# Linear attention and a four-expert MLP: where the late chunks of k are regrouped for VectorE's transpose

## The chip, the cores and the metric

The kernel runs on one core of a Trainium2 chip. The metric is the device time of one execution in microseconds (us). A core has five engines that work side by side, each with an instruction queue of its own that runs in order: TensorE (PE) multiplies matrices, VectorE (DVE) and ScalarE (ACT) do elementwise work and take results out of PSUM, GpSimd (POOL) does elementwise work in SBUF, and SyncE (SP) issues most DMA transfers; ScalarE can issue transfers too. Engines wait for one another, and for transfers, by semaphores.

## The reference

Two stages. The first is linear attention with a decay, over q, k, v of 4 batches, 8 heads, 768 tokens and 64 columns, in blocks of 64 tokens:

```python
for b in range(nb):
    sl = slice(b * block, (b + 1) * block)
    qb, kb, vb = (q[:, :, sl], k[:, :, sl], v[:, :, sl])
    intra = np.einsum('bhic,bhjc->bhij', qb, kb) * Dmask[None]
    intra = np.einsum('bhij,bhjd->bhid', intra, vb)
    inter = np.einsum('bhid,bhde->bhie', qb * lam_pow[None], kv_state)
    out[:, :, sl] = intra + inter
    kb_dec = kb * rev_pow[None]
    kv_state = lam_block[None, :, None, None] * kv_state + np.einsum('bhsd,bhse->bhde', kb_dec, vb)
```

The second takes the result as 3072 tokens of 512 columns through 4 experts (512 to 1024 and back to 512) and weighs their outputs:

```python
p = domain_probs / (domain_probs.sum(-1, keepdims=True) + 1e-09)
for e in range(E):
    h = np.maximum(x @ w1[e], 0.0)
    out += p[:, e:e + 1] * (h @ w2[e])
```

All data are fp32.

## The kernel before

**Tiling and stages.** The tokens go in three groups of 1024 (`NG`), and each group in 8 chunks of 128 tokens, so there are 24 chunks. A pair (group, expert) is a unit, 12 in all. The products of the experts are done by a fast scheme in seven products (`M1` to `M7`), and most of them by seven smaller ones inside. That scheme needs sums and differences of blocks of the weights; GpSimd makes them and stores them in DRAM, and they are loaded again when they are needed. After a start-up of about 100 us, in which the first group's attention and first product are made, the program is a list of steps: unit by unit, seven products in each, eight steps in each product. A step issues two or four pairs of matmuls, what takes their results out of PSUM, and a little of each of several lists.

**The attention of later chunks** is spread over these steps. `attention` (L892) lists for chunks 8 to 23 at which step each part is to be issued; `AT` (L888) holds the step of a chunk's scores. `turn` makes q and k stand with their 64 columns along the partitions, `scores` (L745) makes the products q k and the new state, and `values` (L805) makes the chunk's result, which ScalarE takes out of PSUM (L863) and VectorE completes with a sum. For chunks 8 to 11 `turn` uses TensorE. For the 12 chunks from 12 on (`comes_across`) VectorE does it (`turn_across`, L702): its transpose turns each square of 32 by 32 by itself, so the data must first stand with the right columns in each block of 32 partitions.

**How they come to stand so.** `bring_across` (L490) makes a list of 128 pieces, 32 for each batch: first 16 of q, then 16 of k. A piece is a transfer from DRAM to DRAM that writes 32 columns of one head in runs of 128 bytes; it has 32 KB in the first batch of the list and, for two others, 64 KB. `trickle` issues one piece at a time; in the first unit one in every step, from SyncE in the even steps and from ScalarE's queue in the odd ones, later in the odd steps. `load_across` (L509) loads a chunk's q and k from there into the tiles `qx` and `kx`, and `load` brings k a second time as it is (`kn`), which `decayed` multiplies on GpSimd and `scores` uses for the state. All three loads are issued five steps ahead of the turn.

**The order of the rest.** `send` (L109) issues a transfer and keeps two estimates in steps: `moved`, until when the DMA engines have work, and `asked`, until when SyncE has. `vector` keeps `filled` in the same way for VectorE. `pump` (L208) runs once a step; it begins the next of the `chores` (a load of weights, a sum on GpSimd) only if this holds:

```python
force or free[0] <= now[0] and max(moved[0], asked[0]) < now[0] + FULL and not resting[0]
```

Where a product needs operands that are not made yet, `first_product` (L1131) calls `pump(force=True)` until they are. Among the chores at the end of the start-up are those of the second expert's second weights (`prepare_w2`, L297, called at L1799): a step that loads block B21 and makes the sum T1, one that makes T2, one that makes T4; then come the operands of `M5` (`own_w1`, L1640). Sums and loaded blocks lie in the pool `stage`, which has 7 buffers; an instruction that writes a buffer waits for the readers of what was in it. Tiles such as `qx`, `kx` and `kn` come from a pool of 42 buffers.

## Time and profile before

| | us |
|---|---|
| median of 3 runs | 1142.28 |
| lowest and highest | 1141.87, 1142.56 |
| the profiled execution | 1142.07 |
| its span | 1140.3 |
| TensorE busy in it | 1130.5 |
| GpSimd, VectorE busy | 761.0, 769.0 |
| ScalarE busy | 380.3 |

The span runs from the first instruction of the program to the end of the last; the profiled execution's own time is 1.8 us longer. All times inside the profile count from the start of the span. A busy share is an average over stages: the start-up of about 100 us, the steps with attention until about 500 us, and the rest. In a row of the timeline the first number is the start and the second the length in us, and what stands in brackets is how long the engine had been idle and what released it. Matmuls overlap, so that the duration of one is longer than the distance between two.

### The profile page before, as it was taken

How to read it: one execution, taken by the hardware profiler on the slowest of the kernel's cores; microseconds unless marked ns; L12 is line 12 of the kernel's file. 1: busy time of each engine (PE TensorE's matmuls, PEld its weight loads, DVE VectorE, ACT ScalarE, POOL GpSimd, SP SyncE). 2: the span in 40 equal slices, each digit the busy share in tenths (PEclk: the TensorE clock that was granted, in tenths of full speed). 3: DMA queues.
4: the chain of work that ended last, by engine and by line, in shares of the span. 5: the costliest groups of instructions: out<-in, count | busy, mean ns of one | idle time of the engine just before them, and what ended most of it. 6: DMA issues, size and time to landing. Idle time of an engine off the chain costs nothing.

```text
span 1140.3 us, 22080 instructions
## 1 busy us (share of the span) xinstructions
PE 1130.5 (99%) x7983; PEld 988.2 (87%) x7983; DVE 769.0 (67%) x1474; ACT 380.3 (33%) x768; POOL 761.0 (67%) x730
## 2 busy tenths in 40 slices
PE   8999999999999999999999999999999999999998
PEld 7888888888888888888888888888888888888887
DVE  4576776587577658737655566878767576776785
ACT  3325123212312321232343442444354452342332
POOL 2838147644843786447687997994996873873885
PEclk9999999999999999999999999999999999999999
DMA  9795889999899989769557858886577757657552
GB/s 204 180 287 166 212 222 279 291 270 335 262 292 320 316 291 282 222 222 314 177 177 261 283 180 281 290 272 204 180 264 244 218 162 207 194 160 211 171 194 74
DMA packets 326828, 267.12 MB, mean 234 GB/s; under 512 B 153216, under 2 KB 270144, under 8 KB 326720
## 3 DMA queue, kind: packets, MB, share of 16 engines
q1 hardware_dynamic: 289472, 258.14, 73.1%
q10 hardware_dynamic: 37216, 7.57, 3.5%
q8 instruction: 64, 1.05, 0.4%
q14 instruction: 44, 0.36, 0.1%
q0 software_dynamic: 32, 0.00, 0.0%
HBM read 197.97 MB, written 73.96 MB: 238 GB/s over the span
## 4 chain that ended last, share of the span: by engine, by line
PE 98%; DVE 1%; issue 0%; DMA 0%; ACT 0%; DVEq 0%; POOLq 0%; ACTq 0%
PE pg L1174 41%; PE pq L1550 25%; PE q L1233 21%; PE pM L1692 2%; PE pc L1692 2%; PE op L824 1%; PE sp L761 1%; PE op L842 1%; PE sp L768 1%; PE pM L1417 1%; PE pg L1550 1%; PE qp L727 1%; PE kp L727 0%; DMA decay<-in_lam_dram 0%; PE yp L1377 0%
## 5 line engine op out<-in xcount | busy, mean ns | idle before, releaser
L1174 PE MATMUL pg<-xs,ws_in 128*128 128x256 f32 x1960 | 470.1, 380 | 0.0
L1174 PEld LDWEIGHTS pg<-xs,ws_in 128*128 128x128 f32 x1960 | 371.1, 190 | 52.8 <-DVE m L117 2.4
L117 DVE TENSOR_TENSOR m<-pg,m 128x512 f32<-128x512 f32 x374 | 255.4, 685 | 92.4 <-PE pg L1174 82.5
L1233 PE MATMUL q<-w2t,m 128*128 128x256 f32 x1120 | 265.6, 380 | 0.0
L1233 PEld LDWEIGHTS q<-w2t,m 128*128 128x128 f32 x1120 | 211.7, 190 | 29.3 <-issue 0.3
L117 DVE TENSOR_TENSOR sums<-pq,sums 128x256 f32<-128x256 f32 x272 | 112.9, 420 | 90.6 <-PE pq L1550 76.9
L1550 PE MATMUL pq<-acc,w2t 128*128 128x256 f32 x688 | 169.2, 379 | 0.0
L117 POOL TENSOR_TENSOR m<-m,decay 128x512 f32<-128x512 f32 x91 | 114.5, 1270 | 78.7 <-ACT m L1191 52.1
L1550 PEld LDWEIGHTS pq<-acc,w2t 128*128 128x128 f32 x688 | 130.6, 190 | 17.9
L1191 ACT ACTIVATE m<-m 128x512 f32<-128x512 f32 x99 | 62.4, 630 | 192.5 <-DVE m L117 190.6
L1251 DVE SCALAR_TENSOR_TENSOR acc<-q,gate,acc 128x256 f32<-128x256 f32 x108 | 52.0, 482 | 79.1 <-PE q L1233 78.6
L117 DVE TENSOR_TENSOR m<-m,m 128x512 f32<-128x512 f32 x108 | 92.9, 861 | 6.5 <-ACT m L1157 6.5
L1187 ACT COPY m<-pg 128x512 f32<-128x512 f32 x88 | 51.5, 585 | 122.0 <-PE pg L1174 108.7
L1151 ACT COPY pg<-m 128x512 f32<-128x512 f32 x77 | 45.4, 590 | 113.0 <-DVE m L117 103.3
L117 POOL TENSOR_TENSOR acc<-hT,hT 128x512 f32<-128x512 f32 x56 | 70.3, 1272 | 15.0 <-PE pq L1550 9.9
L117 POOL TENSOR_TENSOR acc<-hT,acc 128x512 f32<-128x512 f32 x56 | 71.2, 1272 | 6.4 <-PE pq L1550 2.7
L1550 PE MATMUL pq<-hT,w2t 128*128 128x256 f32 x288 | 70.0, 379 | 0.0
L117 POOL TENSOR_TENSOR w2o<-w2b 128x512 f32<-128x512 f32 x26 | 33.9, 1325 | 45.8 <-DMA w2b<-in_moe_w_dram 39.3
L1550 PEld LDWEIGHTS pq<-hT,w2t 128*128 128x128 f32 x288 | 54.7, 190 | 7.4
L1155 ACT COPY m<-pg 128x512 f32<-128x512 f32 x44 | 25.7, 585 | 89.6 <-PE pg L1174 84.8
L1550 PE MATMUL pq<-m,w2t 128*128 128x256 f32 x228 | 55.4, 379 | 0.0
L1005 ACT COPY hp<-m 128x512 f32<-128x512 f32 x84 | 48.5, 589 | 15.6 <-DVE hT L117 14.1
(157 smaller groups left out, 1419.5 us busy)
## 6 DMA issues: line engine op xcount, KB each, us to landing
ws_in<-w_ops SPq DMA_DIRECT2D x40, 512.0 KB, 5.1
w2t<-w_ops SPq DMA_DIRECT2D x72, 256.0 KB, 3.2
ws_in<-w_ops SPq DMA_DIRECT2D x60, 256.0 KB, 3.5
ws_in<-w_ops SPq DMA_DIRECT2D x40, 384.0 KB, 4.0
w2b<-in_moe_w_dram SPq DMA_DIRECT2D x56, 256.0 KB, 5.0
w_ops<-ops SPq DMA_DIRECT2D x28, 512.0 KB, 5.5
w_ops<-ops SPq DMA_DIRECT2D x54, 256.0 KB, 4.3
w2t<-w_ops SPq DMA_DIRECT2D x100, 128.0 KB, 2.8
```

The lines of the kernel that those rows point to most:

```text
L117: eng.tensor_tensor(out=o, in0=a, in1=b, op=op)
L727: nc.tensor.transpose(out=x[:, ac * C:(ac + 1) * C], in_=y[:, ac].rearrange("p r d -> p (r d)"), identity=ident[:],)
L1005: nc.scalar.copy(out=there[x][:], in_=blk[at][:])
L1151: nc.scalar.copy(out=banks[tags[1]][:], in_=new["11"][:])
L1155: nc.scalar.copy(out=o[:], in_=p[:])
L1174: nc.tensor.matmul(out=p[:, j * 256:(j + 1) * 256], lhsT=ws[i][:, j * P:(j + 1) * P], rhs=xs[i], start=(fresh and j == 0), stop=True, skip ...
L1187: nc.scalar.copy(out=new[at][:], in_=p[:])
L1191: nc.scalar.activation(out=new[at][:], in_=new[at][:], func=AF.Relu)
L1233: nc.tensor.matmul(out=p[:, s * DH:(s + 1) * DH], lhsT=h[A_OF[m]][:, c * 256 + s * P:c * 256 + (s + 1) * P], rhs=fed2[g, e, m][uu][:, c], ...
L1251: nc.vector.scalar_tensor_tensor(out=o, in0=x, scalar=w, in1=o, op0=ALU.mult, op1=ALU.add)
L1550: nc.tensor.matmul(out=p[:, 0:256], lhsT=fed3[e, m, i][:, c * P:(c + 1) * P], rhs=b[B_OF[i]][:, c * 256:(c + 1) * 256], start=(fresh and c ...
L1692: nc.tensor.matmul(out=p[:, s * 256:(s + 1) * 256], lhsT=a[c][:, f:f + P], rhs=b[:, c, j * 256:(j + 1) * 256], start=(s == 0 and c == 0 an ...
```

## The change

k of the late chunks is no longer copied within DRAM. `bring_across` makes pieces of q alone, 64 in all, and all of them go through SyncE. `load_across` loads `qx` alone. k is loaded as it is, by a step of its own that stands 15 to 18 steps ahead of the turn (`K_AHEAD`), and five steps after that load `regroup` puts 16 copies into a list: ScalarE copies 32 partitions by 4 heads by 32 columns from `kn` to their place in `kx`. Two copies are taken from the list in every step, and `moved_by` issues what is left of a chunk's when its turn comes. `turn_across` adds 0.41 to VectorE's estimate for each transpose in place of what `vector(W, False)` added.

```diff
-    across = dram.tile([2, P, NHP, B, 16, 32], FP32, name="across")
+    across = dram.tile([P, NHP, B, 16, 32], FP32, name="across")
...
-        for x, of in enumerate((q, k)):
-            for y in range(4):
-                for ac in range(NHP):
-                    src = of[b, 4 * (y // 2) + ac, c * C:, (y % 2) * 32:(y % 2 + 1) * 32]
-                    to = across[x, y * 32:(y + 1) * 32, ac, b, (c - 2) * 4:]
...
+        for y in range(4):
+            for ac in range(NHP):
+                src = q[b, 4 * (y // 2) + ac, c * C:, (y % 2) * 32:(y % 2 + 1) * 32]
+                to = across[y * 32:(y + 1) * 32, ac, b, (c - 2) * 4:]
...
     def load_across(n):
         c, b = where(n)
-        for x, name in enumerate("qk"):
-            t = small(f"{name}x")
-            send(
-                out=t[:].rearrange("p (h c) -> p h c", c=C),
-                in_=across[x, :, :, b, (c - 2) * 4:(c - 1) * 4].rearrange("p h t d -> p h (t d)"),
+        t = nat[n, "qx"] = small("qx")
+        send(
+            out=t[:].rearrange("p (h c) -> p h c", c=C),
+            in_=across[:, :, b, (c - 2) * 4:(c - 1) * 4].rearrange("p h t d -> p h (t d)"),
+        )
+
+    moves = []
+
+    def regroup(n):
+
+        of = nat[n, "k"]
+
+        def move(j, x):
+            if (n, "kx") not in nat:
+                nat[n, "kx"] = small("kx")
+            to = nat[n, "kx"][:].rearrange("p (h t c) -> p h t c", h=NHP, c=32)
+            nc.scalar.copy(
+                out=to[j * 32:(j + 1) * 32, :, x],
+                in_=of[x * 32:(x + 1) * 32, :, j // 2, j % 2 * 32:(j % 2 + 1) * 32],
             )
-            nat[n, name + "x"] = t
+
+        moves.extend((n, lambda j=j, x=x: move(j, x)) for j in range(4) for x in range(4))
+
+    def moved_by(n):
+        while any(m <= n for m, _ in moves):
+            moves.pop(0)[1]()
...
             load_across(n)
-            load(n, "k")
...
     def turn_across(n):
 
+        moved_by(n)
...
-            vector(W, False)
+            filled[0] = max(filled[0], now[0]) + 0.41
...
+    K_AHEAD = {14: 16, 15: 17, 16: 17, 18: 16, 20: 18, 22: 16}
...
             if comes_across(n):
+                steps.append((turns_at - K_AHEAD.get(n, 15), lambda n=n: load(n, "k")))
+                steps.append((turns_at - K_AHEAD.get(n, 15) + 5, lambda n=n: regroup(n)))
...
-                if at == 0 or x % 2 or at == 1 and x == 4:
-                    trickle(1, nc.scalar if x % 2 else None)
+                if at == 0 or x % 2:
+                    trickle()
+                for _ in range(2):
+                    if moves:
+                        moves.pop(0)[1]()
```

More of the change, by code (lines that the diff above doesn't have):

```diff
@@ L491, in bring_across @@
         c = min(where(n)[0] for n in range(FIRST_ACROSS, NG * CPG) if where(n)[1] == b)
-        for x, of in enumerate((q, k)):
-            for y in range(4):
-                for ac in range(NHP):
-                    src = of[b, 4 * (y // 2) + ac, c * C:, (y % 2) * 32:(y % 2 + 1) * 32]
-                    to = across[x, y * 32:(y + 1) * 32, ac, b, (c - 2) * 4:]
-                    pieces.append((rank[b], lambda by, to=to, src=src: send(
-                        out=to, in_=src.rearrange("(t p) d -> p t d", p=32), by=by,
-                    )))
+        for y in range(4):
+            for ac in range(NHP):
+                src = q[b, 4 * (y // 2) + ac, c * C:, (y % 2) * 32:(y % 2 + 1) * 32]
+                to = across[y * 32:(y + 1) * 32, ac, b, (c - 2) * 4:]
+                pieces.append((rank[b], lambda by, to=to, src=src: send(
+                    out=to, in_=src.rearrange("(t p) d -> p t d", p=32), by=by,
+                )))
     def trickle(m=1, by=None):
```

## The prediction

> **What bounds the kernel now.** I read the page's busy shares and chain first, then TensorE's waits after its start-up, then the two places that the change reaches: GpSimd around 100 us and ScalarE's queue from 160 to 490 us. On the page:

> ```profile
> span 1140.3 us, 22080 instructions
> ## 1 busy us (share of the span) xinstructions
> PE 1130.5 (99%) x7983; PEld 988.2 (87%) x7983; DVE 769.0 (67%) x1474; ACT 380.3 (33%) x768; POOL 761.0 (67%) x730
> ...
> PE 98%; DVE 1%; issue 0%; DMA 0%; ACT 0%; DVEq 0%; POOLq 0%; ACTq 0%
> ```

> TensorE is the bound: 98% of the chain. TensorE's waits from 60 to 1140 us (total, times, longest) are these two:

> ```profile
> PE sp L761 <- issue: 1.2, 1, 1.2
> PE op L824 <- DVE qT L117: 0.2, 1, 0.2
> ```

> So after start-up there are 1.4 us of idle TensorE to win. The changed program has the same 4052 matmuls in the same order. It can gain at most 1.4 us (0.12%); it can lose wherever a feeding engine becomes late.

> **Added: 192 ScalarE copies (12 chunks of 16, 32 partitions by 128 elements).** Nearest rows, ScalarE by shape from 150 to 500 us, and its timeline around 355 us:

> ```profile
> L863 ACT COPY xc<-op 128x128 f32<-128x128 f32 x60 | 11.4, 277 | 28.3 <-PE op L842 28.2
> ...
> L1155 ACT COPY m<-pg 128x512 f32<-128x512 f32 x13 | 7.6, 585 | 35.4 <-PE pg L1174 30.6 <-DMA across<-in_q_dram 4.8
> ```
> ```profile
> 353.06 0.77 ACT L863 COPY xc<-op 128x128 f32<-128x128 f32 x4 [6.92 <-PE op L842]
> 353.69 0.64 ACT L1151 COPY pg<-m 128x512 f32<-128x512 f32 x1
> 360.26 0.58 ACT L1155 COPY m<-pg 128x512 f32<-128x512 f32 x1 [5.93 <-PE pg L1174]
> ```

> 128 elements take 0.277 us alone, four in a row 0.77, so 0.19 each. 192 copies are 37 us (192 x 0.19) to 53 us (192 x 0.277), in about 310 us where ScalarE is a quarter busy. Out go 67 DMA issues of 0.557 us, 37 us. What covers the copies is the idle ScalarE time, such as the 5.93 us above, and slack behind it: TensorE reuses a bank at least 1.06 us, mostly 1.75 us, after ScalarE has evicted it. In the listed order at most eight copies (1.5 to 2.2 us) stand together; the groups ahead of the seeds at L1151 are of four (0.8 to 1.1 us), against 2.5 us of slack there. What can show is four copies ahead of an L863 eviction whose sum VectorE adds next, with a product sum behind it that TensorE takes within 0.1 us: four or so places of 0.1 us. Ends: 0 (all covered) and 13 us (four uncovered copies, 1.1 us, in each of 12 chunks). I take 0.4 us, near the covered end, because the row has the cover.

> **Moved: k's plain load, 10 to 13 steps earlier.** The copies, and all ScalarE work queued behind them, now wait for its landing: an eviction, then TensorE for the bank. A kn load lands 3.6 to 7.8 us after its issue. The two tightest, at 352 and 452 us, may issue only once an attention product is over (352.5 us); 7.8 us on is 360.3, two copies are 0.4 us, and the next ScalarE work, at 360.26 with over 1 us of slack, loses nothing. Ends 0 and 1 us each; I take 0. VectorE's transposes of k stand 2 to 17 us behind the last copy: 0. The kn buffers are held longer; what newly waits for one waits for matmuls already past.

> **Removed: 64 k pieces in DRAM and 12 loads of kx.** SP loses 39 issues (27 k pieces, 12 kx) and gains 30 (the q pieces that ScalarE's queue had): about 9 x 0.6 us fewer. Less traffic from 170 to 330 us helps loads that TensorE nearly waited for (one vn landed 0.1 us before its use at 268.9 us). The 1.2 us stall at 267.5 us lies beside it, in the fullest stretch of the DMA engines. Ends 0 and 1.4 us; I take all of the 1.2 us row, two chances in three.

> **Moved by the planner: a GpSimd step.** This is where I find the loss. `send` adds a q piece of 64 KB to `moved` where a k piece of 32 KB stood before, so `pump` holds the e=1 step that loads B21 and makes sum T1. In the listing, it and its successors T2 and T4 move from behind the matmuls that ran at 94 to 97 us to behind the one at 102.2 us, where `first_product` forces them because it needs M5's operands. SP then has eight pieces, not four, ahead of the B21 load; still early enough, as in the trace it issues this work 7 us ahead of the matmuls that it stands behind. But T2 asks for its `stage` buffer later and gets the one of M1's `ops`, and with it a wait that it did not have: the last matmul on that tile. No other step on GpSimd has a new wait for TensorE. GpSimd's timeline, then TensorE's:

> ```profile
> 88.38 2.57 POOL L117 TENSOR_TENSOR w2o<-w2b 128x512 f32<-128x512 f32 x2 [5.70 <-DMA w_sums<-w2o]
> 91.03 4.96 POOL L117 TENSOR_TENSOR w2o<-w2b,w2o 128x512 f32<-128x512 f32 x4
> 96.07 1.41 POOL L117 TENSOR_TENSOR ops<-w1o 128x256 f32<-128x256 f32 x2
> ...
> 99.44 2.50 POOL L117 TENSOR_TENSOR w1o<-w1o,w1b 128x512 f32<-128x512 f32 x2 [0.35 <-PE pg L1174]
> ```
> ```profile
> 98.33 1.03 PE L1174 MATMUL pg<-xs,ops 128*128 128x256 f32 x4
> ...
> 102.65 1.03 PE L1174 MATMUL pg<-xs,ops 128*128 128x256 f32 x4
> ```

> T2 and T4 are the four at 91.03; the first `ops` at 96.07 (0.72 us) feeds the matmul at 102.65. The awaited matmul ends at 99.36 (98.33 + 1.03), and GpSimd starts 0.08 us after it, as the 99.44 row shows. From 91.03 to the end of the first `ops` is 96.07 + 0.72 - 91.03 = 5.76 us. So these operands come at 99.44 + 5.76 = 105.20, and with 0.07 us for the wait TensorE resumes at 105.27: 105.27 - 102.65 = **2.6 us lost**. Ends 0 (the wait is over before GpSimd comes to it) and 4 us (the B21 load lands late too). I take 2.6: all its parts are rows. Next in need are the third `ops` (slack 7 us before, still over 1 us) and later ones, which the stall itself gives 2.6 us: nothing.

> **The clock after the stall.** TensorE in four stretches (length, busy, granted clock, DMA):

> ```profile
> 5.68:9.10 3.42, 2.58 (x74) 1.00 1.36 225
> ...
> 12.51:15.92 3.41, 1.31 (x63) 1.00 0.79 218
> 15.92:19.34 3.42, 3.42 (x20) 0.50 0.78 196
> ...
> 265.08:268.49 3.41, 2.38 (x94) 1.00 1.15 350
> ```

> The clock goes by stretches of 3.41 us. After one with 38% busy (1.31 of 3.41) the next ran at 0.50; after 70 and 75% busy it stayed 1.00. A stall of 2.6 us inside one stretch leaves 24% busy; split over two, up to 62%. A stretch at 0.50 costs 3.41 / 2 = 1.7 us. Ends 0 and 1.7; I take 1.7, since most positions of the stall leave a stretch nearer to 38% than to 70%. [...]

> **Sum**, on the profiled execution (1142.07 us, 0.21 below the median 1142.28): 1142.07 + 2.6 + 1.7 + 0.4 - 1.2 = **1145.6 us**, 0.3% above the median. From no change this kernel's runs can tell about 0.2% (2.3 us).

> **Rivals.**
> - [...] 33%: 24 same, 9 slower.
> - *The other side, the GpSimd wait is hidden*: TensorE finds its operands ready. 1142.07 + 0.4 - 1.2 = 1141.3, not slower; it decides if GpSimd starts T2 before 96.8 us (102.65 - 5.83). For: every other wait has slack. Against: the wait is for a matmul that ends at 99.36. 14%: 11 same; 3 faster, if stalls that I don't see go as well.
> - *k lands late*: ScalarE's queue stands at two or more chunks for over 1.75 us. Two stalls of 1 us: 1147.6. For: vn loads took up to 9.5 us. Against: those came with the traffic that is removed. 6%, slower.

> **How the numbers follow.** The forecast has 47%, all slower (1145.6, or 1146.8 with the stall at 267 kept). Slower 47 + 9 + 6 = 62%; same 24 + 11 = 35%; faster 3%. Range: from the hidden wait (1141.3) to 1148.0, the kept stall with late k loads (1146.8 + about 1).

> **What would show it.** Right: a new TensorE idle stretch of some 2.6 us at 102 to 105 us, before an `ops` matmul, released by GpSimd; GpSimd's T2 starting behind TensorE at 99.4 us; a granted clock of 0.50 for 3.4 us after; no wait at L761 near 267 us; ScalarE copies of 0.19 to 0.28 us. Wrong: TensorE idle between 160 and 490 us, above all released by ScalarE or by a kn load; or a span without the gap at 102 us.

## The result and the profile after

The changed kernel takes 1147.69 us in the median (1145.71 to 1151.8, 6 runs) against 1142.07 us before (1140.69 to 1142.78, 6 runs): a ratio of 1.0048, 95% interval 1.0033 to 1.0062. It is slower, by about 5.5 us. The forecast was 1145.6 us. The traced execution took 1149.67 us, 2 us above its median and 7.6 us above the traced one before.

The page of the changed kernel, span, busy time and chain:

```profile
span 1147.9 us, 22213 instructions
## 1 busy us (share of the span) xinstructions
PE 1133.6 (99%) x7983; PEld 989.6 (86%) x7983; DVE 772.4 (67%) x1474; ACT 437.3 (38%) x960; POOL 765.1 (67%) x730
...
PE 93%; SPq 2%; DVE 2%; issue 2%; DMA 1%; POOL 0%; ACT 0%; DVEq 0%; POOLq 0%; ACTq 0%
```

TensorE still has 99% of the span, but 7% of the chain now lies elsewhere. TensorE's waits from 60 us to the end (total, times, longest) name three places that were not there before, and the old 1.2 us at L761 is gone:

```profile
PE pg L1195 <- POOL ops L117: 2.4, 1, 2.4
PE pg L1195 <- DMA ws_in<-w_ops: 2.1, 1, 2.1
PE pg L1195 <- DVE m L117: 0.9, 1, 0.9
PE op L842 <- DVE qT L117: 0.2, 1, 0.2
```

Both kernels have the same 4052 matmuls in the same order, so each matmul's start in one trace can be taken from its start in the other. Worked out so, the delay against the kernel before grows like this:

| place in the changed kernel | delay before and behind it, us | what happens |
|---|---|---|
| 59.5 us | 0.04 | start-up over |
| 105.2 us | 0.04 to 2.58 | TensorE waits for GpSimd's `ops` |
| 105.2 to 108.8 us | 2.58 to 4.28 | half clock (granted 0.50 from 105.41 to 108.82 us) |
| 208.3 us | 4.38 to 5.28 | TensorE waits for VectorE |
| 272.5 us | 5.29 to 7.58 | TensorE waits for a load of `ws_in` |
| 272.5 to 276.4 us | 7.58 to 9.22 | half clock (granted 0.50 from 272.66 to 276.08 us) |
| 276.4 us | 9.22 to 7.79 | the stall before at 267.5 us is not there |
| end | 7.50 | |

**At 102 us** the forecast's line is there. The timelines of GpSimd, then of TensorE:

```profile
99.53 4.95 POOL L117 TENSOR_TENSOR w2o<-w2b,w2o 128x512 f32<-128x512 f32 x4 [7.66 <-issue]
104.45 1.41 POOL L117 TENSOR_TENSOR ops<-w1o 128x256 f32<-128x256 f32 x2
```
```profile
98.37 1.03 PE L1195 MATMUL pg<-xs,ops 128*128 128x256 f32 x4
...
101.82 1.03 PE L1195 MATMUL pg<-xs,w1o 128*128 128x256 f32 x4
105.22 1.93 PE L1195 MATMUL pg<-xs,ops 128*128 128x256 f32 x4 [2.37 <-POOL ops L117]
```

T2 starts 0.13 us behind the matmul that ends at 99.40 (98.37 + 1.03), and TensorE resumes at 105.22; the forecast had 99.44 and 105.27. Four matmuls then take 1.93 us, not 1.03.

**At 270 us** stands what the forecast did not have. SyncE's waits from 240 to 275 us, then its timeline, then the DMA engines from 247 to 273 us (one digit for each 0.65 us, in tenths of their time):

```profile
SPq L114 <- PE op L860: 11.8, 1, 11.8
```
```profile
241.61 3.71 SPq L114 DMA_DIRECT2D w_sums<-w2o  x2
256.73 0.53 SPq L114 DMA_DIRECT2D qx<-across  x1
...
262.72 0.52 SPq L114 DMA_DIRECT2D ws_in<-w_ops  x1
```
```profile
DMA  9710000000000000078899779999999999999996
```

SyncE stands for 11.8 us by this view (11.4 us from the end of its issue before, 245.32, to the start of this one) at the q load of chunk 14, until a matmul that ends at 256.67 us has read what stood in the buffer that this load is to fill, the `qx` of chunk 12. In the kernel before, the same load was issued without such a wait, 3 us ahead of the end of that matmul (251.39 us there):

```profile
248.35 0.55 SPq L114 DMA_DIRECT2D qx<-across  x1
```

In the changed kernel nothing can be issued behind it, so the DMA engines run dry for some 9 us (14 digits of 0), and then everything that has piled up is issued at once. The weights of the matmul at 270 us are the ninth transfer of that pile: issued at 262.72, 7.25 us before TensorE is ready for them, landed at 272.34 after 9.6 us.

**At 208 us** VectorE is late. Its timeline and GpSimd's:

```profile
206.04 1.60 DVE L117 TENSOR_TENSOR qx<-qx,decay 128x512 f32<-128x512 f32 x1
207.56 0.68 DVE L117 TENSOR_TENSOR m<-pg,m 128x512 f32<-128x512 f32 x1
```
```profile
205.82 2.94 POOL L117 TENSOR_TENSOR w1o<-w1o,w1b 128x512 f32<-128x512 f32 x2 [1.11 <-DMA w_ops<-ops]
```

The multiply of `qx` took 0.69 us in the trace before and 1.60 us here, with GpSimd's `w1o` sum beside it. That sum waits for a store to land; before, it began at 204.16 us, when VectorE's work of this stretch was over (203.54). The store took 6.1 us from issue to landing before (landed at 204.09 us) and takes 3.9 us here (205.75 us, where TensorE is 4.38 us later), so that it lands earlier in TensorE's order of work, and GpSimd's sum begins 0.2 us before VectorE's multiply.

### The profile page after: what moved, and what is told of

It is laid out like the page before. It is cut to its first block, busy times and chain, and to the rows that moved or that the text cites. A ratio compares the mean times of both kernels' runs of the same rounds, so it can differ in the third digit from the quotient of the medians.

```text
span 1147.9 us, 22213 instructions
## 1 busy us (share of the span) xinstructions
PE 1133.6 (99%) x7983; PEld 989.6 (86%) x7983; DVE 772.4 (67%) x1474; ACT 437.3 (38%) x960; POOL 765.1 (67%) x730
## 4 chain that ended last, share of the span: by engine, by line
PE 93%; SPq 2%; DVE 2%; issue 2%; DMA 1%; POOL 0%; ACT 0%; DVEq 0%; POOLq 0%; ACTq 0%
PE pg L1195 39%; PE pq L1571 24%; PE q L1254 20%; PE pc L1713 2%; SPq L114 2%; PE pM L1713 1%; PE op L842 1%; PE op L860 1%; PE sp L779 1%; DMA ws_in<-w_ops 1%; PE sp L786 1%; PE pM L1438 1%; PE pg L1571 1%; DVE m L117 0%; PE qp L745 0%
## 5 line engine op out<-in xcount | busy, mean ns | idle before, releaser
L117 DVE TENSOR_TENSOR m<-pg,m 128x512 f32<-128x512 f32 x374 | 255.0, 685 | 95.2 <-PE pg L1195 83.7
L117 DVE TENSOR_TENSOR sums<-pq,sums 128x256 f32<-128x256 f32 x272 | 112.9, 420 | 90.8 <-PE pq L1571 75.3
L117 POOL TENSOR_TENSOR m<-m,decay 128x512 f32<-128x512 f32 x91 | 114.6, 1273 | 86.0 <-ACT m L1212 63.2
L1212 ACT ACTIVATE m<-m 128x512 f32<-128x512 f32 x99 | 62.4, 630 | 161.0 <-DVE m L117 156.4
L117 DVE TENSOR_TENSOR m<-m,m 128x512 f32<-128x512 f32 x108 | 92.7, 858 | 7.5 <-ACT m L1178 6.8
L117 POOL TENSOR_TENSOR acc<-hT,hT 128x512 f32<-128x512 f32 x56 | 70.4, 1272 | 22.6 <-PE pq L1571 13.2
L117 POOL TENSOR_TENSOR acc<-hT,acc 128x512 f32<-128x512 f32 x56 | 71.3, 1273 | 6.6 <-PE pq L1571 2.0
L117 POOL TENSOR_TENSOR w2o<-w2b 128x512 f32<-128x512 f32 x26 | 35.8, 1396 | 42.4 <-DMA w2b<-in_moe_w_dram 30.4
L526 ACT COPY kx<-kn 32x128 f32<-32x128 f32 x192 | 56.7, 295 | 17.8 <-DMA kn<-in_k_dram 8.6
```

Of the source, the lines that this page charges most:

```text
L117: eng.tensor_tensor(out=o, in0=a, in1=b, op=op)
L526: nc.scalar.copy(out=to[j * 32:(j + 1) * 32, :, x], in_=of[x * 32:(x + 1) * 32, :, j // 2, j % 2 * 32:(j % 2 + 1) * 32],)
L1212: nc.scalar.activation(out=new[at][:], in_=new[at][:], func=AF.Relu)
```

## The experiments

The theory after the traces: two buffers are handed out differently, and each brings a wait for TensorE. One is T2's in the `stage` pool (the 102 us stall), the other that of chunk 14's `qx` in the pool of 42 small tiles. The listing of the program shows why the second is short: when that load asks, 41 tiles are live, because k's plain tiles now live 10 to 13 steps longer, and the only free one was released just before. In the kernel before, three were free. The rivals: the copies themselves cost, or SyncE's fuller queue, or the DMA engines are simply full at 270 us. All ratios are to the kernel before, run on the same chip beside the experiments (its medians were 1145.03, 1144.95 and 1145.77 us in the three sets, and its runs spread wider there, from 1140.5 to 1152.6).

### T2's buffer put back

```
-            if pieces:
+            if pieces and not 56 <= now[0] < 68:
                 pieces.pop(0)[1](by)
```

> The changed kernel, with one thing put back: no q piece is handed to SyncE in the steps that run from 88 to 108 us, so that T2's buffer is again that of a tile which nobody on TensorE reads. The copies, the early k loads and everything else stay. If the stall at 102 us is the wait of T2 for TensorE (GpSimd stood 7.66 us ahead of 99.53), the idle 2.5 us there and the 3.4 us at about half clock behind it go together, 2.5 + 1.7 = 4.2 us of the 1147.7, and the kernel takes 1143.5 us (1142.5 to 1145). If the loss is spread over the copies and the fuller SyncE queue, or if the stall moves to the next operand, it stays above 1146.5.

Ratio 0.9993 (0.9974 to 1.0011), 1145.5 us. TensorE's waits from 60 us on:

```profile
PE pg L1195 <- DMA ws_in<-w_ops: 1.4, 1, 1.4
PE pg L1195 <- DVE m L117: 0.9, 1, 0.9
...
PE op L842 <- DVE qT L117: 0.2, 1, 0.2
```

The wait for GpSimd and the half clock at 105 us are gone; the other two stalls stay, the one at 270 us with no half clock behind it. SyncE still stands 10.6 us at the q load. The absolute time is above the expected 1143.5, and above its upper end of 1145, as the kernel before was itself 3 us slower in this set. The ratio alone does not tell this kernel from the one before; the trace does.

### The pool relieved

```
-    K_AHEAD = {14: 16, 15: 17, 16: 17, 18: 16, 20: 18, 22: 16}
+    K_AHEAD = {14: 16, 15: 12, 16: 17, 18: 16, 20: 18, 22: 16}
```

> The changed kernel, with k of one chunk (n = 15) loaded five steps later, so that the buffer pool is not full when the q load of chunk 14 asks for a buffer. If the stall at 270 us comes from SyncE standing 11.8 us at that load (released at 256.67 by a matmul that reads the buffer's last tile), then SyncE issues the weights behind it some 11 us sooner, the 2.3 us of idle TensorE at 270 and the half clock behind it (1.6 us) go, and the kernel takes about 1144 us (1143 to 1146; the stall at 102 is untouched). If that load would have been late anyway, because the DMA engines are full there (a share of 1.06 to 1.08 from 265.8 to 272.6), it stays within 1 us of 1147.7.

Ratio 1.0002 (0.9983 to 1.0022), 1145.93 us. TensorE's waits:

```profile
PE pg L1195 <- POOL ops L117: 2.4, 1, 2.4
PE pg L1195 <- DVE m L117: 0.6, 1, 0.6
PE op L842 <- DVE qT L117: 0.2, 1, 0.2
```

The stall at 270 us and its half clock are gone, the one at 102 us stays with its own. SyncE's longest wait between 238 and 272 us is 2.8 us, and the weights of the matmul at 270 us are issued 15.3 us ahead and land 6.4 us early. SyncE's issues of the q load and of these weights:

```profile
245.95 0.81 SPq L114 DMA_DIRECT2D qx<-across  x1
...
255.01 0.34 SPq L114 DMA_DIRECT2D ws_in<-w_ops  x1
```

The pool is as full as before: by the listing this q load, too, finds 41 live tiles and one free buffer. But that buffer's last reader stands 116 instructions back, not 3. So it is which buffer is free, and not how many, that makes SyncE stand.

### Both

The two edits above, together.

> Both of these edits together. If the two waits for buffers are the whole of the loss, nothing but the copies and the collision of VectorE and GpSimd at 206 us (0.9 us) is left: 1147.7 - 4.2 - 3.9 = 1139.6 by the profiled run's sizes, and not under 1140.7, since the kernel before has only 1.4 us of idle TensorE after its start-up; I expect 1141 to 1142.5. If the copies on ScalarE cost by themselves, TensorE waits for ScalarE somewhere between 160 and 490 us and the time stays over 1143.5.

Ratio 0.9965 (0.9946 to 0.9983), 1142.18 us. TensorE's waits:

```profile
PE pg L1195 <- DVE m L117: 0.6, 1, 0.6
PE op L842 <- DVE qT L117: 0.2, 1, 0.2
```

Neither stall is left, and the kernel is faster than the one before it was run beside. The second time:

> The kernel with both edits a second time, to see whether it is faster than the kernel before: 0.9965 (0.994 to 0.998) if so; 1.000 if the first comparison was luck.

0.9963 (0.9949 to 0.9977), 1141.47 us, with 0.6 us of idle TensorE from 60 us on. So beside these runs the change with both buffers mended is a gain of 0.35%, and the changed kernel lost it, and more, through two buffers. The kernel with both edits was not run where the kernel before took 1142.07 us; how much of the gain is left there is not shown.

### The changed kernel and the one before, again

Both unedited.

> The changed kernel itself, unedited, beside runs of the kernel before on this chip. With the hold of the q pieces worth 0.9965 - 1.0002 = 0.37% and the later k load worth 0.9965 - 0.9993 = 0.28% in the runs with one and with both edits, it should lie at 0.9965 + 0.0037 + 0.0028 = 1.003 of the kernel before (1.001 to 1.006). If the two edits act on one and the same loss, it lies at 1.000.

1.0027 (1.0008 to 1.0045), which fits the sum of the two edits' worths, 0.37% and 0.28%. It is a loose fit: the kernel before, against itself, reads 1.0017 (below). Its trace has the 102 us stall, and no half clock behind it. Windows of 3.41 us (length, then TensorE's busy time; the last three numbers are granted clock, DMA share, GB/s), first trace and this one:

```profile
102.00:105.41 3.41, 1.04 (x5) 0.58 (x5) 2.09 (x5) 0.59 (x1) 3.41 (x5) 1.00 0.56 223
105.41:108.82 3.41, 3.41 (x9) 2.67 (x9) 0.00 (x0) 1.59 (x3) 3.25 (x5) 0.50 0.85 263
```
```profile
99.80:103.21 3.41, 2.72 (x13) 2.06 (x11) 2.04 (x6) 2.18 (x4) 3.41 (x4) 1.00 0.84 305
103.21:106.62 3.41, 1.73 (x8) 1.55 (x9) 0.71 (x2) 0.56 (x2) 3.25 (x5) 1.00 0.67 241
106.62:110.04 3.42, 3.42 (x18) 3.01 (x17) 1.70 (x4) 1.62 (x4) 3.42 (x4) 1.00 1.09 216
```

The same stall of 2.5 us leaves 1.04 of 3.41 us in one window and the next runs at 0.50; split over two windows it leaves 2.72 and 1.73 us, and the clock holds.

> The kernel before, unedited, timed against itself: 1.000 within 0.002. Its trace is wanted. In the first trace TensorE idled 1.4 us from 60 us to the end; its runs beside the experiments spread from 1141.5 to 1152.5 us. If late loads in the full stretch of the DMA engines are what spreads them, this trace shows either the 1.2 us at 267 us again or larger waits for loads between 240 and 280 us. If the spread is all start-up, the offset to the first trace is made before 60 us.

1.0017 (1.0002 to 1.0033), which is what such a comparison shows for no difference at all, so a ratio within 0.2% of 1 tells nothing here. Its trace is not that of the first 1142.07 us: before 60 us the two differ by 0.14 us, and from 60 us on TensorE waits for

```profile
PE pg L1174 <- DMA ws_in<-w_ops: 2.8, 1, 2.8
PE pg L1174 <- DVE m L117: 0.3, 1, 0.3
PE op L824 <- DVE qT L117: 0.2, 1, 0.2
```

at 245 us, with a half clock behind it, and the 1.2 us at L761 is gone. So the kernel before runs with a load that is sometimes late, and its first trace was one of its good executions. Late loads are not all of the spread. By the starts of the same matmuls, at 60 us the other traces lie between 0.9 us ahead of that first trace and 4.7 us behind it (the first one with both edits). From 60 us to the end the four traces of kernels that hold both edits and whose copies are not doubled gain 0.6 to 1.5 us on the first trace of the kernel before, and its own second trace loses 3.2 us on it.

### One part alone: k's load earlier, nothing else

```
             load_across(n)
-            load(n, "k")
...
+                steps.append((turns_at - K_AHEAD.get(n, 15), lambda n=n: load(n, "k")))
```

> The kernel before, with one part of the change alone: k's plain load stands where the change puts it, 10 to 13 steps earlier; the k pieces, the loads of kx and all else stay, and no copy is made. By the listing the pool is then full again and it is the load of kx for chunk 14 that gets the buffer just released by TensorE at 251.4 us. If a full pool is what makes SyncE stand, SyncE waits there for some 5 to 10 us, weights behind it land late, and TensorE stalls near 262 to 270 us: 1143.5 to 1146.5. If the wait does harm only together with the copies or with the q pieces on SyncE's queue, the time is that of the kernel before, 1142.1 within 0.7.

1.0025 (1.0006 to 1.0044), 1149.24 us, so slower, but not by the wait that I expected. SyncE stood only 1.4 us at the load of `kx`; the stalls are a load of `ws_in` at 246 us (2.6 us: SyncE issued it 3.2 us before TensorE was ready, behind more issues), 1.2 us with `issue` as releaser at 272 us and a `vn` at 274 us (0.8 us); a stretch at half clock follows the last two. The first is the stall that the kernel before has in its own second trace (2.8 us, issued 3.4 us ahead), so what the early loads add by themselves is not shown, nor that the buffer alone would do it. What the buffer does is shown by the pair with and without the later k load above.

### What the copies cost

```
-        moves.extend((n, lambda j=j, x=x: move(j, x)) for j in range(4) for x in range(4))
+        moves.extend((n, lambda j=j, x=x: (move(j, x), move(j, x))) for j in range(4) for x in range(4))
```

> The kernel with both edits, and each of its 192 copies made twice in a row, 384 copies. A copy takes 0.295 us in the traces, four in a row 1.22 us, so this is 57 us more on ScalarE between 170 and 490 us, at most four copies (1.2 us) in a step of 1.7 us. If the copies lie in ScalarE's idle time and in the slack of 1.06 us and more behind its evictions, it stays within 0.1% of the kernel with both edits: 0.996 to 0.998 of the kernel before. If ScalarE was already near its limit, TensorE waits for it in each of the 12 chunks, and the ratio is over 1.000.

1.0051 (1.0031 to 1.007), 1151.46 us: a miss. ScalarE by shape from 160 to 490 us in the changed kernel and in this one, and TensorE's waits in this one:

```profile
L526 ACT COPY kx<-kn 32x128 f32<-32x128 f32 x192 | 56.7, 295 | 17.8 <-DMA kn<-in_k_dram 8.6 <-PE op L860 5.1 <-PE q L1254 1.1
```
```profile
L526 ACT COPY kx<-kn 32x128 f32<-32x128 f32 x381 | 112.6, 296 | 19.6 <-DMA kn<-in_k_dram 6.3 <-PE q L1254 4.3 <-ACT gr L650 0.6
```
```profile
PE pg L1195 <- ACT m L1178: 3.9, 5, 1.1
PE op L842 <- ACT gr L650: 1.8, 1, 1.8
PE pg L1195 <- ACT pg L1172: 1.2, 2, 0.8
```

With 16 copies of one chunk TensorE waits for ScalarE behind 60 us in one trace alone, for 0.2 us; with 32 it waits 6.9 us in eight places. The cover is there, but less than twice what the change uses.

```
-        moves.extend((n, lambda j=j, x=x: move(j, x)) for j in range(4) for x in range(4))
+        def at_once():
...
+            nc.scalar.copy(out=nat[n, "kx"][:], in_=of.rearrange("p i r d -> p r i d").rearrange("p r i d -> p (r i d)"))
+
+        moves.append((n, at_once))
```

> The kernel with both edits, but with one copy of 128x512 elements (0.59 us) in place of the 16 small ones (16 x 0.295 = 4.7 us) for each of the 12 chunks. It leaves out the regrouping of k by 32 columns, so its output is not the reference's. If the copies are covered, the time is that of the kernel with both edits within 0.1% (0.9965). If they cost, it is lower by what they cost; my sum put 0.4 us on them.

0.998 (0.9965 to 0.9994), 1142.09 us: no faster than with 16 small copies (0.9965, 0.9963). At their number the copies cost nothing that these runs can tell.

### What moves T2

```
             if pieces:
+                was = moved[0]
                 pieces.pop(0)[1](by)
+                moved[0] = was
```

> The changed kernel, with the q pieces left out of the planner's count `moved`, which the forecast named as what moves the GpSimd step. If the forecast's cause holds, the step goes back, T2 does not wait for TensorE and there is no idle TensorE at 102 us. If instead the order in which the program is listed and its buffers handed out (it goes by an estimate of its own of how long each transfer takes) is what moves, the count is without effect: T2 starts behind the matmul that ends near 99.4 us and TensorE idles 2.5 us, as in the changed kernel.

The count is without effect. The kernel ran once (1150.25 us), so that its trace alone counts. GpSimd's timeline:

```profile
99.48 4.96 POOL L117 TENSOR_TENSOR w2o<-w2b,w2o 128x512 f32<-128x512 f32 x4 [6.50 <-issue]
```

TensorE waits 2.4 us for `ops`, as in the changed kernel. The built programs say the same. T2's tile carries the same running number in the kernel before, in the changed one and in this one, so the planner asks for it at the same place; but in the listing T2 stands behind 693 matmuls in the kernel before, and behind 709 in the other two. TensorE also waits 2.3 us at L781 with `issue` as releaser, which is taken up below.

```
-                    out=to, in_=src.rearrange("(t p) d -> p t d", p=32), by=by,
...
+                half = (16 - (c - 2) * 4) // 2
+                for h in (slice(0, half), slice(half, 2 * half)):
...
+                        out=to[:, h], in_=src.rearrange("(t p) d -> p t d", p=32)[:, h], by=by,
```

> The changed kernel, with each q piece cut into two transfers of half its size, one handed out where a whole one was: 32 KB where the kernel before had a k piece of 32 KB. If the 64 KB size of a piece is what delays the B21 load in the listing, T2 has its old buffer, the idle 2.5 us at 102 us is gone, and what is left is the SyncE wait of some 11 us at the q load of chunk 14 with its stall near 270 us: as with the pieces held back, 0.999 to 1.001 of the kernel before, and twice as many issues on SyncE as the other price. If the number of pieces on SyncE's queue is what delays it, the stall at 102 us stays.

1.0012 (0.9993 to 1.003). The stall at 102 us is gone:

```profile
88.30 2.50 POOL L117 TENSOR_TENSOR w2o<-w2b 128x512 f32<-128x512 f32 x2 [4.54 <-DMA w_sums<-w2o]
90.88 4.96 POOL L117 TENSOR_TENSOR w2o<-w2b,w2o 128x512 f32<-128x512 f32 x4
```

T2 stands behind 688 matmuls in the listing and has its old buffer again. So the forecast had the size right, 64 KB where 32 KB stood, but not what reads it. It is the order in which the program's instructions are listed and its buffers handed out, and not the planner's `moved`; that this order goes by the listing's own estimate of each transfer is what is left, and no run shows it by itself. The other half of the expectation missed: SyncE stood only 1.9 us at the q load, since it was behind with twice the issues, and the weights of the matmul at 270 us were issued 6.3 us ahead and late by 2.1 us all the same. A late load at 270 us thus does not need the wait for a buffer; too little lead on SyncE is enough.

### The q pieces on ScalarE again

```
-                    trickle()
+                    trickle(1, nc.scalar if x % 2 else None)
```

> The kernel with both edits, with the q pieces of the odd steps handed to ScalarE as in the kernel before. SyncE has some 20 issues less (0.6 us each, 12 us), ScalarE 20 more (0.56 us each, 11 us) beside its 57 us of copies. If neither queue bounds the kernel, the ratio is that of the kernel with both edits, 0.9965 within 0.002. If the move of the pieces to SyncE is a gain by itself, it is over 0.999; if it costs, it is under 0.994.

0.9974 (0.9958 to 0.999): no difference from 0.9965 and 0.9963 that these runs can tell. Which of the two queues issues the q pieces makes no difference here.

## Why the prediction was right, and where it was not

The direction, the place of the first loss and the range held; the middle was 2.1 us low. That 1147.69 lies in the range is luck in part: its upper end, 1148.0, was made of late k loads and of a kept stall at 267 us, and neither came. Of the forecast's own signs of being wrong one did come, an idle TensorE between 160 and 490 us (at 208 and at 270 us).

*The GpSimd step, 2.6 us:* measured 2.54, by the mechanism that was worked out (T2 waits for M1's last matmul). The cause ahead of it was wrong: not `moved` and `pump`, but the order in which buffers are handed out.

*The copies, 0.4 us:* nothing. Each took 0.295 us and four in a row 1.22, not 0.19 to 0.277: the row that I took them from reads PSUM, these read SBUF. In the changed kernel's first trace ScalarE's ReLU of 128x512 elements takes 0.63 us from SBUF (L1212) and 0.58 from PSUM (L1178); how much of the difference between 0.277 and 0.295 us is due to that is not shown. The sum was 57 us instead of 37 to 53 and still lay in idle time.

*k's load earlier, 0 us:* this is the step that failed, a term put at nothing. "What newly waits for one waits for matmuls already past" does not hold on SyncE: the q load of chunk 14 newly waits for a matmul that ends 3 us after it was issued before. I priced the wait and not what is queued behind it. SyncE was by then 11 us ahead of TensorE, so the wait was more than 11 us, and the weights behind it came 2.3 us late, 1.6 us of half clock with them: 3.9 us.

*The 1.2 us at 267.5 us:* gone in the changed kernel, but gone in the second trace of the kernel before as well, and there again, with 2.3 and 2.2 us, in two kernels without the traffic of k. So the stall does not need that traffic, and that the term came out was luck.

*Not foreseen:* the 0.9 us for VectorE at 208 us. In five other traces of the changed kernel and its variants the same place has 0.2 to 0.9 us, in the rest nothing. An earlier store let GpSimd begin earlier, beside VectorE.

On the first trace the terms are 2.54 + 1.70 + 0.90 + 2.30 + 1.64 - 1.43 = 7.65 us, against 7.46 measured from 60 us on.

The limit "at most 1.4 us can be won" was read from one execution. It is true of that one; the traces show where the 0.35% come from. How long before TensorE is ready for them two loads of weights are issued, and how late they land (negative: early), us:

| kernel | load at 245 us: ahead, late | load at 265 to 270 us: ahead, late |
|---|---|---|
| before, first trace | 7.2, -1.0 | 9.1, -2.8 |
| before, second trace | 3.4, 3.0 | 12.1, -5.3 |
| changed, first trace | 14.7, -9.4 | 7.2, 2.4 |
| changed, second trace | 14.4, -9.1 | 6.9, 1.3 |
| T2's buffer put back | 13.6, -8.2 | 7.1, 1.6 |
| pool relieved | 12.2, -6.0 | 15.3, -6.4 |
| both, first time | 13.7, -7.6 | 19.0, -8.4 |
| both, second time | 15.0, -9.6 | 18.3, -10.5 |

Without the k pieces SyncE runs ahead, and the load at 245 us, which was early in one trace of the kernel before and late in the other, is safe. The buffer that is released last then takes the lead away from the next one.

## What to carry to other kernels

A tile that is loaded earlier takes a buffer from everyone behind it: look at each request of the pool which buffer it gets and when that buffer's last reader ends, and where one load must wait, price the whole queue behind it by how far that queue was ahead, not by how late the released buffer is. A forecast's floor should not come from one good trace; a load that landed 1.0 us before its use in one execution of the kernel before landed 3.0 us late in another, and a change that moves such loads may be worth more than the idle time shows. Where a stall may halve the clock (here it did behind 1.04 us of work in a window of 3.41, and not behind 1.73), price that by the share of a window that it can leave idle.

## What the runs showed of the hardware

**TensorE's `issue` stalls ended 1.4 to 1.6 us behind an instruction packet.** Queue q8 of kind instruction moves 16 KB packets (64 in an execution). In the four traces with a stall at the same `sp` matmul (1.2, 1.2, 2.3 and 2.2 us) TensorE resumes 1.4 to 1.6 us after the end of such a packet each time (267.1 to 268.63, 271.7 to 273.18, 275.1 to 276.65, 269.5 to 270.97 us); in the ten traces without a stall the last packet had ended 4.4 us or more before that matmul. That the stalls are late instruction fetches is the likely reading, not a shown one. The timeline of the kernel with uncounted pieces:

```profile
273.73 0.63 PE L781 MATMUL sp<-qx,kx 64*64 64x64 f32 x27
276.65 0.34 PE L781 MATMUL sp<-qx,kx 64*64 64x64 f32 x5 [2.29 <-issue]
```

No edit tested it, and what would delay the packet is open.

**VectorE beside GpSimd.** VectorE's 128x512 operation on two SBUF tiles (`m<-m,m`) takes 0.68 us alone. Where GpSimd's sums run beside it for most of its time (60% or more), it takes 0.83 us in the median of 54 cases (first trace of the kernel before) and 0.89 us of 56 (first trace of the changed kernel), and up to 1.79. With one operand in PSUM (`m<-pg,m`, some 250 cases) it takes 0.69 us either way.

**A releaser in a wait need not be the cause.** In the second trace of the changed kernel the 1.1 us at 268 us are put down to VectorE, whose last result for that matmul was ready at 266.25 us; its weights landed at 269.07 us, and the matmul began at 269.20.
